# A spectral filter with a mixture of experts on one core: the first forward step in full precision, the bias as matmuls, an earlier first table

## The chip, the core and the metric

One core of a Trainium2 chip runs the whole kernel in one launch. The metric is device microseconds of that core. In the text TensorE is the matmul engine (PE; PEld is its weight load), VectorE is DVE, ScalarE is ACT, GpSimd is POOL and SyncE is SP, which here only issues DMAs.

## What is computed

The input x is (8, 2496, 256) in float32. The first half is a spectral filter along the sequence, the second a mixture of 8 experts in which each token goes to the one expert of the highest score.

```python
X = np.fft.rfft(x, axis=1)
Yr = Xr @ w_r - Xi @ w_i + b_r
Yi = Xr @ w_i + Xi @ w_r + b_i
Y = soft-threshold of Yr and Yi by 0.01
x = irfft(Y).reshape(19968, 256)
expert = argmax(x @ w_gate);  gate = softmax weight of that expert
out = gate * (relu(x @ w1[expert]) @ w2[expert])      # w1: 256 x 1024, w2: 1024 x 256
```

## The kernel before, in words

The transform of length 2496 = 39 x 64 is done as matmuls in two steps. `fwd_a` (line 279) does the 39-point step: per batch eleven pieces of 117 rows (the last of 78) by 512 columns, whose results `ae` go to a DRAM tensor `spec` and come back turned (`turn`, line 300, tile `t1`). `fwd_b` (line 307) does the 64-point step for one of ten slots of a batch, into PSUM tile `pb`. `halves` (line 317) makes from it the operands of the product with the weights: a high and a low part of float32r type (`sh`, `sl`) of real, imaginary and their sum (`re`, `su`). `mix` (line 333) multiplies by three weight matrices: `pk` (the sum by w_r, shared) and `pm` (two more), six products each since every factor is split into high and low. ScalarE copies `pk` to `k`, GpSimd adds the bias to it (`kb`, line 349), VectorE adds `kb` to `pm` (`v`, line 355). `shrink` (line 358) is the threshold: `r` on ScalarE, four operations `y` on VectorE. `inv_b` (line 374, products `pv`, copies `z`) and `inv_a` (line 387, products `pz`, copies `zh` and `zl`, products `py`, copies `yb`) turn it back; `inv_a` also multiplies by the gate matrix.

Splitting a float32 value means: `xh` is its copy in float32r (ScalarE), `xl` the rest (VectorE); a product of two split values is high by high, low by high, high by low. For batch 0, `fwd_a` takes x and its matrix in float32 as they are; for the others `split_x` (line 269) prepares `xh` and `xl` one slot ahead, and three products follow.

The loop of `spectral` (line 454) goes over 80 slots, ten per batch. In it the order of TensorE, SyncE, ScalarE and VectorE is the order of the program; before it, in the prologue, only that of TensorE and SyncE is, and ScalarE's and VectorE's are chosen by the framework. GpSimd's is chosen by the framework throughout. Slot `it` holds: `fwd_b` and `halves` of slot it+1, `shrink` of slot it-1, `mix` of its own, some `fwd_a` of the next batch (lists `first` and, for the split, `second`), loads of x, and the inverse: `inv_b` from the list `back`, and in slots 2 to 5 of a batch ("turning") three `inv_a` each of the batch before. The inner function `inverse` is called three times in a slot.

Routing is drawn in small steps: `route` (line 558) and `table` (line 638) are generators, and `tick(n)` advances the one at the head of the list `jobs` by n steps. Each step ends at a `yield`. A `route` handles half a batch: logits, argmax, softmax weight, a running count by expert (`scan`, `sb`), a product `pr` with a triangular matrix for the count over rows (line 604), then positions `pos`; its rows go out to the DRAM tensor `xs` by indirect DMAs on GpSimd (`scatter`, line 621), a few per slot by `send`, paced by a dependence on `self.paced`. Between `sb` and `pr` stand four empty steps.

`table` makes the list of tiles of 256 rows, each with its expert. Table 0 is for the first five tiles (EARLY) and is drawn in the last batch after the rows of all batches but one have been counted; table 1 has the rest. SyncE reads them as registers (line 734) for the loads of the experts' weights (line 772) and rows. `finish_last` (line 531) does the inverse of the last batch, with the weights of the first tile being split meanwhile, and tiles 0 to 2 with the remaining routing; `experts_rest` does the others.

Of the kernel before, what the change touches and what calls it, by code (L numbers as in the profile page):

```python
# [10 lines left out]
F32 = mybir.dt.float32  # L11
# [87 lines left out]
class Kernel:  # L99
    def __init__(self, tc, nb, x, w_r, w_i, b_r, b_i, w_gate, w1, w2,  # L100
# [6 lines left out]
        done = (nb - 1) * S  # L107
# [72 lines left out]
    def open_forward(self, st):  # L180
# [8 lines left out]
        self.fh = f.tile([117, 120], F32R, name="fh")  # L189
        self.fl = f.tile([117, 120], F32R, name="fl")  # L190
        self.fer = f.tile([78, 120], F32, name="fer")
        self.feh = f.tile([78, 120], F32R, name="feh")
        self.fel = f.tile([78, 120], F32R, name="fel")
# [4 lines left out]
        self.bias = f.tile([128, 2, D], F32, name="bias")  # L198
# [9 lines left out]
        self.raw = raw  # L208
        for h, b in ((0, self.b_r), (1, self.b_i)):
            nc.gpsimd.dma_start(self.bias[:, h, :], b.rearrange("(o n) -> o n", o=1).broadcast_to((128, D)))  # L210
# [25 lines left out]
    def split_constants(self):  # L236
        nc, f, raw = self.nc, self.f, self.raw
        nc.scalar.copy(self.fh, self.far)
        nc.vector.tensor_sub(self.fl, self.far, self.fh)
        nc.scalar.copy(self.feh, self.fer)  # L240
        nc.vector.tensor_sub(self.fel, self.fer, self.feh)
# [4 lines left out]
        raw = {"r": raw["r"], "d": wd, "s": ws}  # L246
        for nm in ("s", "d", "r"):
            self.wh[nm] = f.tile([128, 2, D], F32R, name="wh" + nm)
            self.wl[nm] = f.tile([128, 2, D], F32R, name="wl" + nm)
            nc.scalar.copy(self.wh[nm], raw[nm])  # L250
            nc.vector.tensor_sub(self.wl[nm], raw[nm], self.wh[nm])
# [17 lines left out]
    def split_x(self, b, q, g):  # L269
        nc = self.nc  # L270
        m = 117 if q < 5 else 78
        xt = self.xg[b, q][:m, g:g + 2, :].rearrange("p g d -> p (g d)")
        xh = self.w.tile([117, 512], F32R, tag="xh", name="xh")
        xl = self.w.tile([117, 512], F32R, tag="xl", name="xl")
        nc.scalar.copy(xh[:m, :], xt)  # L275
        nc.vector.tensor_sub(xl[:m, :], xt, xh[:m, :])  # L276
        self.xs2[b, q, g] = xh, xl

    def fwd_a(self, b, q, g):
        nc = self.nc  # L280
        m = 117 if q < 5 else 78
        raw, hi, lo = (self.far, self.fh, self.fl) if q < 5 else (self.fer, self.feh, self.fel)
        p = self.psi.tile([128, 512], F32, tag="u", name="pa", bufs=4)
        if b:
            xh, xl = self.xs2.pop((b, q, g))
            parts = ((hi, xh), (lo, xh), (hi, xl))
        else:
            parts = ((raw, self.xg[b, q][:, g:g + 2, :].rearrange("p g d -> p (g d)")),)
        for i, (a, v) in enumerate(parts):
            nc.tensor.matmul(p[:120, :], a[:m, :], v[:m, :], start=i == 0, stop=i == len(parts) - 1)  # L290
        ae = self.xp.tile([120, 2, D], F32, tag="ae", name="ae", bufs=5)
# [41 lines left out]
    def mix(self, b, s):  # L333
# [3 lines left out]
        def product(nm, slot, to):  # L337
            i = 0
            for c in range(2):
                for a, ww in ((sh, self.wh), (sh, self.wl), (sl, self.wh)):  # L340
                    nc.tensor.matmul(to, a[:, c, slot, :], ww[nm][:, c, :], start=i == 0, stop=i == 5)
# [6 lines left out]
        kb = self.w.tile([128, 2, D], F32, tag="kb", name="kb", bufs=1)  # L348
        self.paced = nc.gpsimd.tensor_tensor(out=kb, in0=self.bias, in1=k.unsqueeze(1).broadcast_to((128, 2, D)), op=ALU.add)  # L349
# [5 lines left out]
        nc.vector.tensor_add(u, p, kb)  # L355
# [55 lines left out]
    def spectral(self, fwd):  # L411
        nb = self.nb
        self.t1s, self.pbs, self.ss, self.us, self.ys, self.hl, self.xs2 = {}, {}, {}, {}, {}, {}, {}
# [23 lines left out]
        first, second, loads, back = ({i: [] for i in range(-1, n)} for _ in range(4))  # L437
        for b in range(1, nb):
            at = 10 * b - 10
            for i, o in enumerate((1, 1, 2, 2, 3, 3, 4, 4, 5, 5, 6) if b == 1 else (-3, -2, -1, 0, 0, 1, 2, 3, 4, 5, 6)):  # L440
                first[at + o].append((b, *pairs[i]))
                second[at + o - 1].append((b, *pairs[i]))
# [11 lines left out]
        for it in range(n):  # L454
            b, s = todo[it]
            late = b == nb - 1
            half, small = iter(()), iter(())
            if it + 1 < n:
# [3 lines left out]
            if it:  # L462
                small = self.shrink(*todo[it - 1])
                next(small)
            next(half, None)
# [503 lines left out]
```

## Time and profile before

| what | value |
|---|---|
| median of 3 runs | 1668.5 us (1666.49 to 1670.34) |
| the profiled execution | 1668.7 us |
| its span, first to last instruction | 1666.9 us |
| mean granted TensorE clock | 0.974 |
| TensorE busy | 1534.7 us (92%) |
| VectorE busy | 1335.3 us (80%) |
| ScalarE busy | 1116.1 us (67%) |
| GpSimd busy | 617.5 us (37%) |

The span is the time from the first to the last instruction of the program; the execution's own time has 1.8 us around it. Busy TensorE time is the union of matmuls that overlap and whose ends are modelled. Times of rows below are microseconds from the start of the span; a row of a timeline has start, duration, engine, line, operation, result and operands, shape, count, and in brackets the idle time of the engine before it and who ended it.

### The profile page before, as it was taken

How to read it: one execution, taken by the hardware profiler on the slowest of the kernel's cores; microseconds unless marked ns; L12 is line 12 of the kernel's file. 1: busy time of each engine (PE TensorE's matmuls, PEld its weight loads, DVE VectorE, ACT ScalarE, POOL GpSimd, SP SyncE). 2: the span in 40 equal slices, each digit the busy share in tenths (PEclk: the TensorE clock that was granted, in tenths of full speed). 3: DMA queues.
4: the chain of work that ended last, by engine and by line, in shares of the span. 5: the costliest groups of instructions: out<-in, count | busy, mean ns of one | idle time of the engine just before them, and what ended most of it. 6: DMA issues, size and time to landing. Idle time of an engine off the chain costs nothing. (4 is left out here: it accounts for less than half of the span.)

```text
span 1666.9 us, 36023 instructions
## 1 busy us (share of the span) xinstructions
PE 1534.7 (92%) x10880; PEld 1422.8 (85%) x10880; DVE 1335.3 (80%) x2755; ACT 1116.1 (67%) x2334; POOL 617.5 (37%) x462
## 2 busy tenths in 40 slices
PE   5889898988988887779999999999999999999997
PEld 2778787878878886778999999999999999999996
DVE  2678878888888888668888888888888888888886
ACT  2677777676767665546677677677677667677675
POOL 2121626362535345351333333333333333333332
PEclk8899999999999998999999999999999999999998
DMA  8753535353535311324322312312312313213210
GB/s 249 200 145 94 171 98 161 108 156 107 164 95 148 102 57 46 114 65 102 97 50 46 99 47 46 100 46 60 85 46 61 83 46 96 49 46 91 52 46 19
DMA packets 182932, 153.81 MB, mean 92 GB/s; under 512 B 120378, under 2 KB 154080, under 8 KB 182477
## 3 DMA queue, kind: packets, MB, share of 16 engines
q1 hardware_dynamic: 162829, 107.17, 25.6%
q0 software_dynamic: 19904, 44.29, 8.1%
q8 instruction: 88, 1.44, 0.4%
q14 instruction: 111, 0.91, 0.2%
HBM read 243.33 MB, written 66.37 MB: 186 GB/s over the span
## 5 line engine op out<-in xcount | busy, mean ns | idle before, releaser
L892 POOL DMA_INDIRECT out<-o,row x154 | 303.7, 1972 | 571.2 <-DVE o L890 546.1
L882 PE MATMUL po<-h,hh 128*128 128x512 f32 x1312 | 463.4, 397 | 2.7 <-ACT hh L849 2.7
L844 PE MATMUL ph<-xh,l 128*128 128x256 f32 x1312 | 372.0, 284 | 4.4 <-DVE l L785 4.4
L844 PE MATMUL ph<-xh,h 128*128 128x256 f32 x1312 | 372.4, 284 | 0.6 <-ACT h L784 0.5
L844 PE MATMUL ph<-xl,h 128*128 128x256 f32 x1312 | 371.8, 283 | 0.2 <-DVE xl L827 0.2
L849 ACT ACTIVATE hh<-ph 128x512 fp32r<-128x512 f32 x328 | 196.0, 598 | 251.9 <-PE ph L844 232.5
L850 DVE SCALAR_TENSOR_TENSOR hl<-ph,hh 128x512 fp32r<-128x512 f32 x328 | 226.7, 691 | 150.6 <-ACT hh L849 136.5
L879 PE MATMUL po<-h,hl 128*128 128x256 f32 x1148 | 322.6, 281 | 0.2 <-DVE hl L850 0.2
L882 PEld LDWEIGHTS po<-h,hh 128*128 128x128 f32 x1312 | 242.2, 189 | 47.4 <-ACT hh L849 3.0
L844 PEld LDWEIGHTS ph<-xh,l 128*128 128x128 f32 x1312 | 251.9, 192 | 8.4 <-DVE l L785 4.9
L844 PEld LDWEIGHTS ph<-xh,h 128*128 128x128 f32 x1312 | 251.4, 192 | 1.4 <-ACT h L784 0.7
L844 PEld LDWEIGHTS ph<-xl,h 128*128 128x128 f32 x1312 | 251.9, 192 | 0.4 <-DVE xl L827 0.4
L349 POOL TENSOR_TENSOR kb<-bias,k 128x512 f32<-128x512 f32 x80 | 106.1, 1326 | 332.8 <-ACT k L347 289.8
L879 PEld LDWEIGHTS po<-h,hl 128*128 128x128 f32 x1148 | 217.9, 190 | 4.5 <-DVE hl L850 0.5
L624 POOL DMA_INDIRECT xs_dram<-yb,pos x176 | 182.8, 1039 | 82.4 <-issue 43.6
L785 DVE TENSOR_TENSOR l<-r,h 128x512 fp32r<-128x512 f32 x332 | 206.8, 682 | 3.1 <-ACT h L784 3.0
L800 DVE TENSOR_TENSOR h<-r,h 128x512 fp32r<-128x512 f32 x332 | 206.9, 684 | 2.8 <-ACT h L799 2.8
L784 ACT CAST h<-r 128x512 fp32r<-128x512 f32 x332 | 180.7, 618 | 1.8 <-DMA r<-moe_w 1.8
L799 ACT CAST h<-r 128x512 fp32r<-128x512 f32 x332 | 180.4, 618 | 0.0
L368 DVE SCALAR_TENSOR_TENSOR y<-v,r 64x256 f32<-64x256 f32 x320 | 159.7, 499 | 6.1 <-issue 0.8
L381 PE MATMUL pv<-bi,y 128*128 128x128 f32 x640 | 95.3, 288 | 22.5 <-DVE y L368 20.9
L276 DVE TENSOR_TENSOR xl<-x,xh 117x512 fp32r<-117x512 f32 (+1 forms) x77 | 70.4, 926 | 56.5 <-ACT xh L275 54.7
(190 smaller groups left out, 2927.9 us busy)
## 6 DMA issues: line engine op xcount, KB each, us to landing
r<-moe_w SPq DMA_DIRECT2D x178, 512.0 KB
r<-moe_w SPq DMA_DIRECT2D x632, 128.0 KB
spec_dram<-ae SPq DMA_DIRECT2D x88, 240.0 KB
t<-spec_dram SPq DMA_DIRECT2D x160, 128.0 KB
xq<-xs_dram SPq DMA_DIRECT2D x312, 64.0 KB
x<-x SPq DMA_DIRECT2D x40, 384.0 KB
x<-x SPq DMA_DIRECT2D x40, 84.0 KB
xs_dram<-yb,pos POOLq DMA_INDIRECT x176
```

What stands on the lines that cost most here:

```text
L368: nc.vector.scalar_tensor_tensor(out=y[q * 64:q * 64 + 64, kp, :], in0=u[h, q, :], scalar=LAM, in1=r[h, q, :], op0=ALU.add, op1=ALU.min)
L624: i = nc.gpsimd.indirect_dma_start(out=self.xs[:, :], out_offset=bass.IndirectOffsetOnAxis(ap=pos[:n, g:g + 1], axis=0), in_=y[:n, g, 0:XW ...
L784: nc.scalar.copy(hi[:, c, s], v)
L785: nc.vector.tensor_sub(lo[:, c, s], v, hi[:, c, s])
L799: nc.scalar.copy(hi[:, s, :], v)
L800: nc.vector.tensor_sub(lo[:, s, :], v, hi[:, s, :])
L844: nc.tensor.matmul(p[:, i, :], a[:, c, f * 128:(f + 1) * 128], v[:, c, :], start=m == 0, stop=m == 5)
L849: nc.scalar.activation(hh[:, s, :], p, AF.Relu)
L850: nc.vector.scalar_tensor_tensor(out=hl[:, s, :], in0=p, scalar=0.0, in1=hh[:, s, :], op0=ALU.max, op1=ALU.subtract)
L879: nc.tensor.matmul(p[:, :D], hl[:, f - 1, hs], w2[:, f - 1, 0, :], start=False, stop=False)
L882: nc.tensor.matmul(p, hh[:, f, hs], w2[:, f].rearrange("p a d -> p (a d)"), start=f == 0, stop=f == 7)
L892: i = nc.gpsimd.indirect_dma_start(out=self.out[:, :], out_offset=bass.IndirectOffsetOnAxis(ap=at[h], axis=0), in_=o[:, h, :], in_offset=N ...
```

## The change

`fwd_a` takes float32 operands for every batch; `split_x`, its list `second` and the split matrices go. The bias is added by TensorE: `self.bias` becomes float32r with the high part in row 0 and the rest in row 32 of 128 rows, all else zero, and in `mix` a product of `self.ones` (128 x 128 of ones) with it opens each of the two groups of `pm`. `k` is added by VectorE as it is; GpSimd copies one element of it as a mark for the pacing. `ae` has eight buffers in place of five. In turning slots the first `inverse()` of the slot is called ahead of `shrink` and of the second half of `halves`. Table 0 is drawn from all batches but two, from slot 1 of the last batch on in place of slot 6. Between `sb` and `pr` stand five empty steps, in the last batch ten; ahead of the last product of table 1 four in place of one.

```diff
@@ -104,7 +104,7 @@
         self.ntok = nb * S
         self.cap = TT + self.ntok
         self.nt = (self.ntok + E * (TT - 1)) // TT
-        done = (nb - 1) * S
+        done = (nb - 2) * S
         self.early = EARLY if done - E * (TT - 1) > (EARLY - 1) * TT else 0
         self.spec = [self.nc.dram_tensor(f"spec{i}_dram", (120, G, D), F32, kind="Internal").ap() for i in range(2)]
         self.xs = self.nc.dram_tensor("xs_dram", (E * self.cap, XW), F32, kind="Internal").ap()
@@ -186,16 +186,13 @@
         self.psf = self.pool(st, "psf", 1, side="right", space=PSUM)
 
         self.far = far = f.tile([117, 120], F32, name="far")
-        self.fh = f.tile([117, 120], F32R, name="fh")
-        self.fl = f.tile([117, 120], F32R, name="fl")
         self.fer = f.tile([78, 120], F32, name="fer")
-        self.feh = f.tile([78, 120], F32R, name="feh")
-        self.fel = f.tile([78, 120], F32R, name="fel")
         nc.sync.dma_start(far, self.c_fa)
         nc.sync.dma_start(self.fer, self.c_fe)
         self.bm = f.tile([128, K1, 128], F32, name="bm")
         self.bi = f.tile([128, K1, 128], F32, name="bi")
-        self.bias = f.tile([128, 2, D], F32, name="bias")
+        self.bias = f.tile([128, 2, D], F32R, name="bias")
+        self.ones = f.tile([128, 128], F32R, name="ones")
         self.xg = {}
         for q in range(6):
             self.load_x(0, q)
@@ -206,8 +203,10 @@
             nc.sync.dma_start(raw[nm], src.rearrange("(c p) n -> p c n", p=128))
         self.wh, self.wl = {}, {}
         self.raw = raw
+        self.braw = self.w.tile([33, 2, D], F32, tag="y", name="braw", bufs=6)
         for h, b in ((0, self.b_r), (1, self.b_i)):
-            nc.gpsimd.dma_start(self.bias[:, h, :], b.rearrange("(o n) -> o n", o=1).broadcast_to((128, D)))
+            for q in (0, 32):
+                nc.gpsimd.dma_start(self.braw[q:q + 1, h, :], b.rearrange("(o n) -> o n", o=1))
         self.nlam = f.tile([128, 1], F32, name="nlam")
         nc.vector.memset(self.nlam, -LAM)
 
@@ -235,15 +234,19 @@
 
     def split_constants(self):
         nc, f, raw = self.nc, self.f, self.raw
-        nc.scalar.copy(self.fh, self.far)
-        nc.vector.tensor_sub(self.fl, self.far, self.fh)
-        nc.scalar.copy(self.feh, self.fer)
-        nc.vector.tensor_sub(self.fel, self.fer, self.feh)
         ws = self.w.tile([128, 2, D], F32, tag="r", name="wsum")
         wd = self.w.tile([128, 2, D], F32, tag="r", name="wdif")
         nc.vector.tensor_sub(wd, raw["i"], raw["r"])
         nc.vector.scalar_tensor_tensor(out=ws, in0=raw["i"], scalar=-1.0, in1=raw["r"], op0=ALU.mult, op1=ALU.subtract)
         raw = {"r": raw["r"], "d": wd, "s": ws}
+        zero = self.w.tile([128, 2, D], F32, tag="y", name="zero", bufs=6)
+        nc.vector.memset(zero, 0.0)
+        nc.vector.tensor_copy(self.bias, zero)
+        nc.vector.tensor_scalar_add(self.ones, zero[:, 0, 0:128], 1.0)
+        bh = self.w.tile([33, 2, D], F32R, tag="y", name="bh", bufs=6)
+        nc.scalar.copy(self.bias[0:1], self.braw[0:1])
+        nc.scalar.copy(bh[32:33], self.braw[32:33])
+        nc.vector.tensor_sub(self.bias[32:33], self.braw[32:33], bh[32:33])
         for nm in ("s", "d", "r"):
             self.wh[nm] = f.tile([128, 2, D], F32R, name="wh" + nm)
             self.wl[nm] = f.tile([128, 2, D], F32R, name="wl" + nm)
@@ -266,29 +269,13 @@
             self.nc.sync.dma_start(t[lo * j:hi * j, :n, :].rearrange("p g d -> p (g d)"), src)
         self.xg[b, q] = t
 
-    def split_x(self, b, q, g):
+    def fwd_a(self, b, q, g):
         nc = self.nc
         m = 117 if q < 5 else 78
-        xt = self.xg[b, q][:m, g:g + 2, :].rearrange("p g d -> p (g d)")
-        xh = self.w.tile([117, 512], F32R, tag="xh", name="xh")
-        xl = self.w.tile([117, 512], F32R, tag="xl", name="xl")
-        nc.scalar.copy(xh[:m, :], xt)
-        nc.vector.tensor_sub(xl[:m, :], xt, xh[:m, :])
-        self.xs2[b, q, g] = xh, xl
-
-    def fwd_a(self, b, q, g):
-        nc = self.nc
-        m = 117 if q < 5 else 78
-        raw, hi, lo = (self.far, self.fh, self.fl) if q < 5 else (self.fer, self.feh, self.fel)
         p = self.psi.tile([128, 512], F32, tag="u", name="pa", bufs=4)
-        if b:
-            xh, xl = self.xs2.pop((b, q, g))
-            parts = ((hi, xh), (lo, xh), (hi, xl))
-        else:
-            parts = ((raw, self.xg[b, q][:, g:g + 2, :].rearrange("p g d -> p (g d)")),)
-        for i, (a, v) in enumerate(parts):
-            nc.tensor.matmul(p[:120, :], a[:m, :], v[:m, :], start=i == 0, stop=i == len(parts) - 1)
-        ae = self.xp.tile([120, 2, D], F32, tag="ae", name="ae", bufs=5)
+        nc.tensor.matmul(p[:120, :], (self.far if q < 5 else self.fer)[:m, :],
+                         self.xg[b, q][:m, g:g + 2, :].rearrange("p g d -> p (g d)"), start=True, stop=True)
+        ae = self.xp.tile([120, 2, D], F32, tag="ae", name="ae", bufs=8)
         to = ae.rearrange("p g d -> p (g d)")
         if b == 0 and g:
             nc.vector.tensor_copy(to, p[:120, :])
@@ -335,24 +322,25 @@
         sh, sl = self.ss.pop((b, s))
 
         def product(nm, slot, to):
-            i = 0
+            i = 0 if nm == "r" else 1
+            if i:
+                nc.tensor.matmul(to, self.ones, self.bias[:, 1 if nm == "d" else 0, :], start=True, stop=False)
             for c in range(2):
                 for a, ww in ((sh, self.wh), (sh, self.wl), (sl, self.wh)):
-                    nc.tensor.matmul(to, a[:, c, slot, :], ww[nm][:, c, :], start=i == 0, stop=i == 5)
+                    nc.tensor.matmul(to, a[:, c, slot, :], ww[nm][:, c, :], start=i == 0, stop=i == (5 if nm == "r" else 6))
                     i += 1
 
         pk = self.psi.tile([128, 512], F32, tag="yo", name="pk")
         product("r", 2, pk[:, :D])
         k = self.w.tile([128, D], F32, tag="k", name="k", bufs=1)
         nc.scalar.copy(k, pk[:, :D])
-        kb = self.w.tile([128, 2, D], F32, tag="kb", name="kb", bufs=1)
-        self.paced = nc.gpsimd.tensor_tensor(out=kb, in0=self.bias, in1=k.unsqueeze(1).broadcast_to((128, 2, D)), op=ALU.add)
+        self.paced = nc.gpsimd.tensor_copy(self.mark, k[0:1, 0:1])
         yield
         p = self.psf.tile([128, 2, D], F32, tag="m", name="pm", bufs=1)
         product("d", 0, p[:, 1, :])
         product("s", 1, p[:, 0, :])
         u = self.w.tile([128, 2, D], F32, tag="v", name="v")
-        nc.vector.tensor_add(u, p, kb)
+        nc.vector.tensor_add(u, p, k.unsqueeze(1).broadcast_to((128, 2, D)))
         self.us[b, s] = u
 
     def shrink(self, b, s):
@@ -410,7 +398,7 @@
 
     def spectral(self, fwd):
         nb = self.nb
-        self.t1s, self.pbs, self.ss, self.us, self.ys, self.hl, self.xs2 = {}, {}, {}, {}, {}, {}, {}
+        self.t1s, self.pbs, self.ss, self.us, self.ys, self.hl = {}, {}, {}, {}, {}, {}
         self.jobs, self.rows = [], []
         pairs = [(q, g) for q in range(6) for g in ((0, 2) if q < 5 else (0,))]
         todo = [(b, s) for b in range(nb) for s in range(10)]
@@ -434,12 +422,11 @@
         for _ in self.halves(*todo[0]):
             pass
 
-        first, second, loads, back = ({i: [] for i in range(-1, n)} for _ in range(4))
+        first, loads, back = ({i: [] for i in range(n)} for _ in range(3))
         for b in range(1, nb):
             at = 10 * b - 10
             for i, o in enumerate((1, 1, 2, 2, 3, 3, 4, 4, 5, 5, 6) if b == 1 else (-3, -2, -1, 0, 0, 1, 2, 3, 4, 5, 6)):
                 first[at + o].append((b, *pairs[i]))
-                second[at + o - 1].append((b, *pairs[i]))
             for q, o in enumerate((None, None, 0, 1, 1, 2) if b == 1 else (-7, -5, -4, -2, 0, 2)):
                 if o is not None:
                     loads[at + o].append((b, q))
@@ -455,15 +442,11 @@
             b, s = todo[it]
             late = b == nb - 1
             half, small = iter(()), iter(())
+            turning = b and 2 <= s < 6
             if it + 1 < n:
                 self.fwd_b(*todo[it + 1])
                 half = self.halves(*todo[it + 1])
                 next(half)
-            if it:
-                small = self.shrink(*todo[it - 1])
-                next(small)
-            next(half, None)
-            turning = b and 2 <= s < 6
             turns = iter(range(3 * s - 6, 3 * s - 3) if turning else ())
 
             def inverse():
@@ -474,8 +457,15 @@
                     break
 
             spare = 1 if late else 0
+            if turning:
+                inverse()
+            if it:
+                small = self.shrink(*todo[it - 1])
+                next(small)
+            next(half, None)
             self.tick(2 + spare)
-            inverse()
+            if not turning:
+                inverse()
             mix = self.mix(b, s)
             if not turning:
                 next(mix)
@@ -484,8 +474,6 @@
             if turning:
                 next(mix)
             next(small, None)
-            for a in second[it]:
-                self.split_x(*a)
             self.tick(2 + spare)
             inverse()
             next(small, None)
@@ -500,7 +488,7 @@
                 self.write_blank()
             if it + 4 < n:
                 self.turn(*todo[it + 4])
-            if late and self.early and s == 6:
+            if late and self.early and s == 1:
                 self.jobs.append(self.table(0))
         for _ in self.shrink(*todo[n - 1]):
             pass
@@ -598,7 +586,7 @@
         pa = pa[:, 8:, :]
         sb = small("sb", (117, E), BF16)
         nc.vector.tensor_copy(sb, pa[:, GH - 1, :])
-        for _ in range(4):
+        for _ in range(10 if b == self.nb - 1 else 5):
             yield
         p = self.psi.tile([128, 512], F32, tag="yo", name="pr")
         nc.tensor.matmul(p[:117, :E], self.ltri, sb, start=True, stop=False)
@@ -709,7 +697,8 @@
         if last:
             lap = rt.tile([128, 128], F32, name="lap")
             nc.vector.tensor_copy(lap, fin[:, 3:4].broadcast_to((128, 128)))
-            yield "pe"
+            for _ in range(4):
+                yield
             p = self.psi.tile([128, 512], F32, tag="yo", name="pl")
             nc.tensor.matmul(p[:, 0:128], lap, self.ident, start=True, stop=True)
             for h in range(2):
```

## Rows read from the trace of the kernel before

**Rows 1.** Busy time by stage, one row for each stretch: the stretch, its length, then busy us (and instructions) of PE, PEld, DVE, ACT, POOL, the granted clock, the DMA engines' busy share and GB/s.

```profile
0.00:100.00 100.00, 73.71 (x395) 54.55 (x396) 49.01 (x106) 47.49 (x101) 22.12 (x36) 0.90 0.73 214
100.00:578.00 478.00, 418.63 (x3174) 394.33 (x3173) 393.89 (x947) 337.79 (x823) 202.50 (x178) 0.97 0.45 128
578.00:672.00 94.00, 76.83 (x566) 71.80 (x565) 74.29 (x203) 51.95 (x125) 49.23 (x46) 0.92 0.18 56
672.00:757.00 85.00, 68.68 (x441) 62.40 (x441) 56.29 (x160) 44.34 (x103) 34.70 (x46) 0.90 0.28 85
757.00:1667.00 910.00, 896.87 (x6312) 839.75 (x6309) 761.87 (x1340) 634.51 (x1185) 308.95 (x159) 1.00 0.27 64
416.00:422.00 6.00, 5.69 (x28) 5.69 (x28) 4.49 (x11) 3.29 (x9) 4.28 (x4) 0.50 0.62 175
```

**Rows 2.** Waits of PE from 100 to 578 us: who waited for whom, us in total, times, the longest.

```profile
PE pr L604 <- DVE sb L600: 23.0, 6, 3.9
PE pk L341 <- ACT yb L407: 10.9, 18, 1.1
PE pv L381 <- DVE y L368: 10.9, 13, 1.6
PE pz L392 <- DVE zl L398: 7.3, 6, 1.2
PE py L406 <- DVE zl L398: 4.4, 6, 0.7
PE py L406 <- ACT yb L407: 1.8, 6, 0.3
```

**Rows 3.** Timeline of PE from 396 to 425 us.

```profile
404.28 0.28 PE L341 MATMUL pk<-wlr,sh 128*128 128x256 f32 x1
404.40 0.28 PE L341 MATMUL pk<-whr,sl 128*128 128x256 f32 x1
...
404.88 0.40 PE L290 MATMUL pa<-xh,fh 117*120 117x512 f32 x1
...
405.58 1.05 PE L381 MATMUL pv<-bi,y 128*128 128x128 f32 x8
...
407.91 1.06 PE L313 MATMUL pb<-bm,t 128*128 128x128 f32 x8
...
416.31 0.17 PE L604 MATMUL pr<-sb,ltri 117*117 117x8 bf16 x1 [3.94 <-DVE sb L600]
...
417.01 0.41 PE L341 MATMUL pm<-whd,sl 128*128 128x256 f32 x1
417.22 0.41 PE L341 MATMUL pm<-whd,sh 128*128 128x256 f32 x1
```

**Rows 4.** Timeline of all engines from 411 to 418 us, the rows of y, v and kb.

```profile
411.76 0.86 DVE L368 SCALAR_TENSOR_TENSOR y<-v,r 64x256 f32<-64x256 f32 x2
...
413.27 0.63 DVE L355 TENSOR_TENSOR v<-pm,kb 128x512 f32<-128x512 f32 x1
...
416.17 1.87 DVE L368 SCALAR_TENSOR_TENSOR y<-v,r 64x256 f32<-64x256 f32 x2
...
416.46 1.29 POOL L349 TENSOR_TENSOR kb<-bias,k 128x512 f32<-128x512 f32 x1 [2.07 <-ACT k L347]
```

**Rows 5.** Groups of instructions from 100 to 578 us, shapes apart: count, busy us, mean ns of one, idle us of the engine before them and what ended it.

```profile
L368 DVE SCALAR_TENSOR_TENSOR y<-v,r 64x256 f32<-64x256 f32 x242 | 119.0, 492 | 3.4
L349 POOL TENSOR_TENSOR kb<-bias,k 128x512 f32<-128x512 f32 x61 | 80.7, 1323 | 232.5 <-ACT k L347 193.4 <-DVE y L368 35.2 <-issue 3.1
...
L384 ACT COPY z<-pv 128x256 f32<-128x256 f32 x118 | 69.0, 704 | 0.0
...
L276 DVE TENSOR_TENSOR xl<-x,xh 117x512 fp32r<-117x512 f32 x58 | 52.6, 915 | 41.7 <-ACT xh L275 39.9 <-ACT ae L297 1.3
```

**Rows 6.** Timeline of all engines from 0 to 62 us, the prologue.

```profile
8.71 1.95 PE L290 MATMUL pa<-x,far 117*120 117x512 f32 x4 [0.93 <-DMA x<-x]
...
25.06 0.62 ACT L250 CAST whr<-wraw 128x512 fp32r<-128x512 f32 x1 [8.52 <-DMA wraw<-w_r]
...
26.92 0.68 DVE L294 COPY ae<-pa 120x512 f32<-120x512 f32 x1
...
27.66 2.06 PE L290 MATMUL pa<-x,far 117*120 117x512 f32 x2 [6.73 <-DVE ae L294]
```

**Rows 7.** Waits of PE from 0 to 100 us.

```profile
PE pv L381 <- DVE y L368: 9.0, 7, 3.5
```

**Rows 8.** Waits of PE from 578 to 757 us.

```profile
PE pr L604 <- DVE sb L600: 6.5, 2, 4.1
PE ph L844 <- DVE l L785: 4.0, 1, 4.0
...
PE pq L706 <- DVE fin L700: 2.9, 1, 2.9
...
PE pl L714 <- DVE lap L711: 2.1, 1, 2.1
```

**Rows 9.** Timelines of DVE, POOL and SP between 660 and 770 us: the second table, the last row sent to `xs`, the first load that needs both.

```profile
728.55 0.67 DVE L708 CAST tab<-pq 1x512 int32<-1x512 f32 x1
...
747.11 0.91 POOL L624 DMA_INDIRECT xs_dram<-yb,pos  x1 [0.18 <-issue]
...
756.81 1.98 SPq L749 DMA_DIRECT2D xq<-xs_dram  x4
```

## The prediction

> **What bounds the kernel now.** I began with busy time by stage [rows 1]. From 757 to 1667 us, the experts, TensorE is busy 897 of 910 us at clock 1.00, and the diff issues nothing there: that stage keeps its length. Everything lies in the 757 us before. From 100 to 578 us (six batches of some 80 us) TensorE is busy 419 of 478 us, VectorE 394, and the granted clock is 0.97, so 14 us are lost to half clock. Busy matmuls overlap and say little of where TensorE stands still; its list of waits does [rows 2]: per batch one wait of up to 3.9 us for the VectorE cast sb (line 600), then smaller ones for y, yb and zl.
>
> The timeline of TensorE [rows 3] shows what the long wait costs. pr starts at 416.31 us after 3.94 us of idling. Behind it the 256-column products of mix follow each other at 0.21 us (417.01 to 417.22) where it was 0.12 us (404.28 to 404.40): from 416 to 422 us the granted clock is 0.50 [rows 1], 1.2 in place of 2.4 GHz, and the engine had stood idle before the fall. Such a stall is paid nearly twice.
>
> Why is sb late? VectorE executes in order, and it is behind: v, the last step of a slot, starts at 413.27 us [rows 4], though TensorE had gone on to the next slot's pb at 407.91 us [rows 3], 5 us before. Two things hold VectorE up. First, the split of x [rows 5]: xl takes 0.915 us (58 times), and VectorE idles 41.7 us in front of it, because xh on ScalarE stands behind k and ae, which wait for TensorE; together 1.6 us per slot. Second, kb on GpSimd: the pair of y at 416.17 us took 1.87 us, the pair at 411.76 us 0.86 us; beside the slow pair kb ran from 416.46 us for 1.29 us [rows 4]. Over the stage y takes 0.492 us in the mean [rows 5] against 0.43 us (0.86 / 2) without kb: 242 x 0.06 = 15 us.
>
> **The change, part by part.** The sum goes against the profiled execution, 1668.7 us around a span of 1666.9 us; it agrees with the median of the three runs, 1668.5 us.
>
> *Full precision in place of three products.* A split product is three matmuls, 404.88 to 405.58 us, 0.70 us [rows 3]. The full-precision one of batch 0 is two instructions of TensorE: four of them take 1.95 us with the tail of the last [rows 6], so some 0.45 us each and 0.91 us a product, an estimate from that row. Added: 0.21 us for 77 products (11 per batch from 1 to 7), 16 us. Removed per product: xh, xl and the idling before it. An x tile is held one slot longer, until fwd_a; loads into its buffer are issued three slots or more after that, so SyncE's queue waits for nothing new.
>
> *Bias by products.* Two 256-column products of 0.12 us (a spacing that holds each one's weight load) in 80 slots: 19 us on TensorE. kb leaves GpSimd (1.32 us per slot [rows 5]) and the path to v. The 1x1 copy that takes its place as pacing has no row in this stage; it costs between nothing and kb's time, on an engine busy 203 of 478 us [rows 1], and holds up scatters alone.
>
> So TensorE gets 35 us more work, for certain: 20 x 0.12 + 11 x 0.21 = 4.7 us before 100 us, 120 x 0.12 + 64 x 0.21 = 27.8 us from 100 to 578, 2.4 us from 578 to 672. Against it stand the stalls.
>
> *Prologue and batch 0 (to 100 us).* TensorE stands 6.7 us, to 27.66 us, for the sixth ae, which VectorE copied only at 26.92 us, after weight work that waited for ScalarE's copy of 25.06 us [rows 6]. These two engines have no order by hand here; with five buffers the sixth ae has to wait for a store, with eight it has not. I take 5 of the 6.7 us; at worst nothing, since the new order isn't visible. The preparation of zero, ones and bias (some six short instructions) lies in VectorE's idle time before the weights; without that cover it costs 2 us. Two more small DMAs on GpSimd stand in front of loads that nothing needs early. The waits of pv for y (9.0 us [rows 7]) shrink when y stands behind xl no longer: 6 us. Net 4.7 - 5 - 6 = -6.3 us (bounds +5 and -11).
>
> *100 to 578 us.* pr waits 23.0 us [rows 2]. Each slot frees VectorE of xl, of its wait and of part of kb, some 2 us, against a lag of 5 us that grew over several slots; and pr is drawn one step later. I take all of it, 11 of the 14 us of half clock and 8 of the 10.9 us for y. The waits in the slots with the inverse step (10.9 + 1.8 for yb, 7.3 + 4.4 for zl, together 24.4 us) hang on a chain of copies that stays. The first inverse piece now stands ahead of r and sh on ScalarE and of sl on VectorE; it has no DMA, and what it passes has the rest of the slot. I take 9 us. Net 27.8 - 23 - 11 - 8 - 9 = -23.2 us (bounds +28 and -46). What is late next: those copies, and z on ScalarE, four of 0.70 us in the slots with two inverse products [rows 5].
>
> *578 to 672 us.* pr 4.1 us, pq 2.9 us [rows 8], half clock 7.5 us (0.08 of 94 [rows 1]). The early table, all VectorE and TensorE work, moves ahead of batch 6's routing into slots 2 and 3, where VectorE has zl to make: I take 4.1 + 1.5 + 5 us and give back 2 for a new wait there (between nothing and pq's 2.9). Net 2.4 - 10.6 + 2 = -6.2 us (bounds +5 and -12).
>
> *672 to 757 us.* Half clock 8.5 us, the second pr 2.4, pl 2.1, ph 4.0 us [rows 8]. Six more empty steps ahead of pr and three ahead of pl take these two waits away, 4.5 us, and some 4 us of half clock. Behind them the last rows and the second table come some 6 us later. Their cover: the table was ready at 729.2 us, the last row went out at 747.11 us, the first load that needs both at 756.81 us [rows 9]. If that doesn't cover it, it costs up to 3 us; I take 1.5. Net -7 us (bounds +3 and -17).
>
> Sum: -6.3 - 23.2 - 6.2 - 7 = -42.7 us, **1626 us**.
>
> **The rivals.** *More comes back (0.15).* If every kb (61 in the stage, 80.7 us) holds VectorE up for its whole length, several times the 15 us that I count is freed, and the rest of the waits of rows 2 goes too: 15.4 + 2.9 + 3 = 21 us, 1605 us. For it speaks the 1.87 us pair; against it the mean of y, and that kb often falls beside other work. The Trainium skill (SBUF — State Buffer, section Who interferes with whom) says that a VectorE operation with two inputs in SBUF and a GpSimd operation that reads SBUF block each other for a whole instruction. The slow pair agrees with that rule; by it alone the sum would be this rival's.
>
> *The inverse slots set the pace (0.18).* If copies to zl and yb hold TensorE whatever VectorE is spared, those 9 us stay, and with them half of the relief in clock and y (10 us); the prologue keeps its order (5 us), and the last two stages give half (7 us): 1657 us.
>
> *Slower (0.12).* sb is late not for the split but for v, r, y and the routing steps ahead of it in VectorE's order; 394 busy of 478 us speak for it, the 5 us lag that starts at xl's waits against. Then pr keeps its wait and its half clock, the 35 us come on top with 2 for the moved table, and only y (14 us) and the end (3 us) give: 1668.7 + 35 + 2 - 17 = 1689 us. It decides if under 35 us of the some 110 us of stalls named above go.
>
> *The early table does nothing:* the first weights' loads may wait for the last inverse product and not for the table. That is in the sum already, at nought, and moves no chance.
>
> **How the numbers follow.** The forecast has 0.51, the rivals 0.15, 0.18 and 0.12; 0.04 is left within 0.2% (3.3 us, about what a measurement of this kernel can tell from no change). Faster: 0.51 + 0.15 + 0.18 = 0.84. The forecast's own bounds are 1607 to 1647 us. Left out are the far end of the first rival, below 1600 us (0.07), and the slower case, above 1668 us (0.12).
>
> **What would show it.** Right: waits of pr under 1 us; clock 0.99 from 100 us to the end of batch 6, and some 76 us a batch; no wait of pa for ae; v within 2 us of the next pb; y at 0.43 us. Wrong: a wait of pr over 2 us, a wait of several us per batch under another name, or an expert stage of another length than 910 us.

## The result and the profile after

The changed kernel takes 1593.4 us (median of 4 runs, 1589.29 to 1596.27) where the kernel before took 1669.4 in the same session: ratio 0.9544, 95% interval 0.9515 to 0.9572. It is faster by 76 us; 43 were predicted, and the time lies below the range. The profiled execution took 1596.3 us around a span of 1594.4.

Busy time by stage of the kernel after, columns as in [rows 1]. The cuts are events of the work: the first pb of batch 1, the first pb of batch 7, the last pb, the first ph of the experts.

```profile
0.00:88.40 88.40, 71.85 (x399) 52.51 (x400) 41.63 (x97) 40.44 (x87) 15.47 (x38) 0.90 0.79 239
88.40:520.70 432.30, 421.91 (x3230) 388.15 (x3229) 319.14 (x880) 306.09 (x756) 134.07 (x175) 0.99 0.48 141
520.70:592.50 71.80, 61.18 (x486) 58.09 (x485) 56.16 (x182) 43.55 (x110) 26.50 (x34) 0.98 0.19 58
592.50:633.90 41.40, 34.77 (x266) 31.47 (x265) 27.71 (x73) 29.04 (x75) 14.81 (x18) 1.00 0.41 124
633.90:1594.40 960.50, 941.34 (x6591) 879.27 (x6589) 800.68 (x1452) 658.61 (x1232) 338.22 (x198) 0.99 0.26 65
```

In the kernel before the same cuts lie at 100.0, 578.0, 650.2 and 701.5 us. So the stretches changed by -11.6, -45.7, -0.4, -9.9 and -4.9 us: three fifths of the gain are in batches 1 to 6. There TensorE is busy 422 of 432 us at clock 0.99 (before: 419 of 478 at 0.97 [rows 1]) and VectorE 319, no longer 394. TensorE's waits in that stretch (who waited for whom, us in total, times, the longest) answer to [rows 2]:

```profile
PE py L394 <- ACT k L336: 4.8, 6, 1.0
PE pz L380 <- DVE zl L386: 3.7, 1, 3.7
PE pm L327 <- DVE v L343: 1.1, 1, 1.1
PE pr L592 <- DVE scan L582: 0.7, 1, 0.7
```

Before, these waits were 59.4 us, 58.3 of them in [rows 2]. There is left 0.7 for pr and nothing for y or yb; a new one is py for ScalarE's copy k, 0.8 us a batch, and the single zl is a disturbance told of at the end. VectorE's lag itself is gone: v started more than 2 us behind the pb that opens the next slot in 29 of the 60 slots of batches 1 to 6 before, now in 5. The groups of that stretch, as in [rows 5]: y takes 418 ns where it took 492, and GpSimd's 1x1 copy 0.30 us where kb took 1.32.

```profile
L356 DVE SCALAR_TENSOR_TENSOR y<-v,r 64x256 f32<-64x256 f32 x239 | 99.8, 418 | 3.3
...
L337 POOL COPY mark<-k 1x1 f32<-1x1 f32 x59 | 17.9, 303 | 248.2 <-ACT k L336 244.6 <-issue 3.6
```

### The profile page after: what moved, and what is told of

Read it like the earlier page. It is cut to its first block, busy times and chain, and to the rows that moved or that the text cites. A ratio compares the mean times of both kernels' runs of the same rounds, so it can differ in the third digit from the quotient of the medians.

```text
span 1594.4 us, 35844 instructions
## 1 busy us (share of the span) xinstructions
PE 1531.1 (96%) x10963; PEld 1409.5 (88%) x10963; DVE 1245.3 (78%) x2680; ACT 1077.7 (68%) x2257; POOL 529.1 (33%) x462
## 4 chain that ended last, share of the span: by engine, by line
issue 41%; PE 32%; POOL 18%; DVE 4%; ACT 2%; DMA 2%; POOLq 0%; SPq 0%; another core or an unknown queue 0%; DVEq 0%; ACTq 0%
POOL out L881 17%; PE pm L330 7%; PE pz L380 5%; PE pb L300 4%; PE pv L369 4%; PE py L394 4%; PE pa L276 4%; PE pk L330 3%; PE pm L327 1%; DMA wraw<-w_r 1%; POOL xs_dram L612 1%; DVE y L356 0%; DMA x<-x 0%; POOLq L881 0%; ACT yb L395 0%
## 5 line engine op out<-in xcount | busy, mean ns | idle before, releaser
L881 POOL DMA_INDIRECT out<-o,row x154 | 299.0, 1942 | 577.3 <-DVE o L879 537.4
L337 POOL COPY mark<-k 1x1 f32<-1x1 f32 x80 | 24.4, 305 | 356.1 <-ACT k L336 352.5
L356 DVE SCALAR_TENSOR_TENSOR y<-v,r 64x256 f32<-64x256 f32 x320 | 133.7, 418 | 6.1 <-ACT r L350 1.6
L313 DVE TENSOR_TENSOR su<-re,pb 128x256 f32<-128x256 f32 x80 | 33.7, 421 | 93.5 <-ACT sh L312 49.4
L380 PE MATMUL pz<-iw,z 128*120 128x136 f32 x704 | 97.1, 281 | 4.5 <-DVE zl L386 3.7
```

What stands on the lines that cost most here:

```text
L380: nc.tensor.matmul(p[:120, c * 136:(c + 1) * 136], self.z[:, c, 3 * g:3 * g + 3, :].rearrange("p j a -> p (j a)"), self.iw[:, c, :], start ...
L881: i = nc.gpsimd.indirect_dma_start(out=self.out[:, :], out_offset=bass.IndirectOffsetOnAxis(ap=at[h], axis=0), in_=o[:, h, :], in_offset=N ...
```

## The experiments

In the table, "batches 1 to 6" is the time from the first pb of batch 1 to that of batch 7 in the profile. A time in the column "before there" holds for the rows down to the next one: these kernels ran on one chip. The last column is the ratio to the kernel before on that chip.

| kernel | median us | before there | batches 1 to 6 | ratio |
|---|---|---|---|---|
| after (the result) | 1593.4 | 1669.4 | 432.3 | 0.9544 |
| e1 fp32 alone | 1615.7 | 1667.8 | 436.5 | 0.9685 |
| e2 bias alone | 1657.3 | | 464.1 | 0.9925 |
| e3 after, kb back | 1605.9 | | 437.5 | 0.9618 |
| e4 after, idle addition | 1613.4 | | 444.1 | 0.9668 |
| e5 after, old order | 1578.5 | 1662.2 | 424.6 | 0.9504 |
| e6 after, pr as before | 1587.7 | | 424.6 | 0.9555 |
| e7 after, late table | 1571.2 | | 423.7 | 0.9459 |
| e8 after, five ae | 1578.3 | | 423.4 | 0.9491 |
| e9 after again | 1595.2 | 1666.9 | 431.1 | 0.9562 |
| e10 both parts alone | 1618.8 | | 432.6 | 0.9724 |
| e11 bias on VectorE | 1599.5 | | 430.0 | 0.9598 |
| e12 after, idle memset | 1595.4 | | 431.3 | 0.9578 |
| e13 after, third time | 1577.4 | 1661.9 | 423.7 | 0.9484 |
| e14 after, late table | 1573.0 | | 423.7 | 0.9462 |
| e15 after, old order | 1576.9 | | 424.6 | 0.9491 |
| e16 both parts alone | 1597.3 | | 429.5 | 0.9601 |

**One part at a time (e1, e2).**

```diff
 # e1: the kernel before, with fwd_a of the kernel after
-            for a in second[it]:
-                self.split_x(*a)
 # e2: the kernel before, with the bias of the kernel after
-        self.paced = nc.gpsimd.tensor_tensor(out=kb, in0=self.bias, in1=k..., op=ALU.add)
+        self.paced = nc.gpsimd.tensor_copy(self.mark, k[0:1, 0:1])
```

> The kernel before with one part of the change alone: the first forward step in full precision, no split of x; kb, the order of the slot, the buffers of ae and the places of the table and of pr stay as before. Theory V (VectorE's lag comes from xl and from its waiting for xh; once that is gone TensorE sets the pace): most of the gain comes with this part, pr waits fall from 23 us to under 5 us in batches 1 to 6, batches of 72 to 74 us, about 1610 us. Theory K (kb on GpSimd holds VectorE up and delays v): the waits stay, 16 us of products are added and some 15 to 30 come back, 1650 to 1670 us. If the new order in the slots with the inverse step is what removed yb's and zl's waits, those waits (24 us) stay here.

> The kernel before with the other part alone: the bias by two products per slot, kb gone, a 1x1 copy as the mark; x is still split. Theory V: TensorE gets 19 us more, y and v come earlier by what kb cost (15 us), the lag behind xl stays: 1655 to 1680 us with waits of pr near 20 us. Theory K: the waits go with kb, y takes 0.42 us, about 1620 us.

e1 gave 52 us, e2 10.6, both near the times of theory V; but pr keeps 12.4 us in e1, where under 5 were expected, and in e2 y falls to 420 ns while 17.3 us of pr's waits stay, so theory K alone fell. TensorE's waits in batches 1 to 6, first e1:

```profile
PE pr L578 <- DVE sb L574: 9.9, 5, 3.4
PE pk L317 <- ACT yb L383: 9.9, 18, 1.6
PE pr L578 <- DVE scan L568: 2.5, 1, 2.5
PE py L382 <- ACT yb L383: 0.6, 1, 0.6
```

and e2:

```profile
PE pr L616 <- DVE sb L612: 15.3, 5, 3.1
PE pk L354 <- ACT yb L419: 9.7, 18, 1.1
PE pv L393 <- DVE y L380: 3.9, 10, 1.1
PE pz L404 <- issue: 3.9, 5, 0.8
PE pr L616 <- issue: 2.0, 1, 2.0
PE pz L404 <- DVE zl L410: 0.8, 1, 0.8
```

Either part takes away the waits for zl (11.7 us [rows 2]; 0.8 left in e2, beside 3.9 us of pz for which the profile shows no cause); those for yb stay near 10 us with either part alone. Against the added work, 64 x 0.16 = 10 us in e1 and 120 x 0.12 = 14 us in e2, the stretch of 478 us lost 41.5 and 13.9 us. So 52 and 28 us of stalls went, together 80. In kernels with both parts and nothing else (e10 and e16, below) 70 and 73 us go, so the two reliefs add up but for a tenth. e2 also shows a price that the prediction missed:

```profile
L287 DVE TENSOR_TENSOR xl<-x,xh 117x512 fp32r<-117x512 f32 x58 | 39.6, 692 | 44.4 <-ACT xh L286 39.7 <-ACT ae L308 4.4
```

Without kb xl takes 692 ns where it took 915 [rows 5].

**What kb did (e3, e4, e12).**

```diff
 # e3: bias and kb as in the kernel before, all else as after
 # e4: the kernel after, plus
+        self.paced = nc.gpsimd.tensor_tensor(out=kb, in0=self.bm[:, 0:4, :]..., in1=k..., op=ALU.add)
-        self.paced = nc.gpsimd.tensor_copy(self.mark, k[0:1, 0:1])
 # e12: the kernel after, plus
+        nc.gpsimd.memset(idle, 0.0)
```

> The kernel after with kb back on GpSimd in place of the two bias products; all else as after. Theory V: VectorE has room now (busy 320 of 433 us in batches 1 to 6), TensorE loses 19 us of products: 1575 to 1590 us, faster than the kernel after. Theory K: y goes back to 0.49 us or more and v comes later; waits of pr or py for VectorE come back, 1615 us or more.

> The kernel after plus one GpSimd addition per slot, as long as kb and with two operands in SBUF, whose result nothing reads (it takes the place of the 1x1 copy and paces the scatters). It shows what GpSimd beside VectorE costs without kb's place on the way to v. Theory K by blocking: VectorE loses up to 80 x 1.3 us, y over 0.49 us, and the time grows by 15 us or more. Theory V, or theory K by the way to v alone: within 5 us of the kernel after, though y may take 0.49 us.

> The kernel after plus one GpSimd memset of 128x512 per slot, right behind the 1x1 copy, into a tile that nothing reads: GpSimd is busy as with the idle addition but reads nothing from SBUF. If GpSimd's reading is what stops VectorE's operations with both inputs in SBUF: y keeps its 0.42 us and the time is that of the kernel after within 3 us. If any work of GpSimd stops them: y near 0.59 us and 15 us or more slower.

e3 lies between its two theories: 1605.9 us, where 1575 to 1590 or 1615 and more were expected. TensorE has 19 us less to do than in the kernel after and still the time is 12.5 us longer; y takes 591 ns and pr waits 11.4 us in batches 1 to 6 again.

Theory K held in its second form: an addition that nobody reads costs 20 us (1613.4 against 1593.4; here chips differ, but their kernels before by 1.6 us only). y in batches 1 to 6 of e4:

```profile
L358 DVE SCALAR_TENSOR_TENSOR y<-v,r 64x256 f32<-64x256 f32 x241 | 139.6, 579 | 3.3
```

The timeline of e4 shows which operations are stopped:

```profile
301.50 1.82 DVE L358 SCALAR_TENSOR_TENSOR y<-v,r 64x256 f32<-64x256 f32 x2
301.77 1.28 POOL L338 TENSOR_TENSOR kb<-bm,k 128x512 f32<-128x512 f32 x1 [1.62 <-ACT k L336]
...
351.29 1.28 POOL L338 TENSOR_TENSOR kb<-bm,k 128x512 f32<-128x512 f32 x1 [7.61 <-ACT k L336]
...
351.30 0.24 DVE L572 TENSOR_REDUCE mx<-lg 117x11 f32<-117x88 f32 x1
...
351.58 1.02 DVE L573 TENSOR_SCALAR mx<-mx 117x11 f32<-117x11 f32 x1
...
352.52 0.77 DVE L388 TENSOR_TENSOR zl<-pz,zh 120x272 fp32r<-120x272 f32 x2
```

The reduction runs beside the addition in its 0.24 us. The next operation, 11 elements wide, ends at 352.60, when the addition does (352.57). Over the run the 209 y that touch no addition take 418 ns, the 111 that do 910 ns with 686 ns of overlap. That mean again mixes two kinds: 54 of the 111 keep 0.42 us, nearly all of them begun before the addition; the other 57 take 1.38 us in the mean and end 0.28 us behind the addition. The pair at 301.50 us has one of each. The 20 zl with an overlap take 432 ns, as the others do: zl reads one operand from PSUM, y both from SBUF. The Trainium skill (SBUF — State Buffer, section Who interferes with whom) has this rule: two SBUF inputs contend with a GpSimd instruction that reads SBUF and block for its whole length; a reduction does not. The trace agrees for y, zl and the reduction, with the limit that a y begun first mostly runs through. The 11-element operation has one SBUF input and is held all the same, which this rule does not cover.

e12 bears on the other half of that rule. The framework moved all 80 memsets into the first 67 us, so it does not show one per slot, and its time (1595.4 beside 1595.2 us in e9) says nothing of the rule; but where they ran beside y, y kept 0.43 us each (1.73 for four):

```profile
48.00 8.69 POOL L339 MEMSET kb<- 128x512 f32 x15
...
52.92 1.73 DVE L358 SCALAR_TENSOR_TENSOR y<-v,r 64x256 f32<-64x256 f32 x4
```

GpSimd that only writes stopped nothing here.

**The small edits, one undone at a time (e5 to e8).**

```diff
 # e5
-            if turning:
-                inverse()
 # e6
+        for _ in range(4):
-        for _ in range(10 if b == self.nb - 1 else 5):
 # e7
-            if late and self.early and s == 1:      # and done = (nb - 2) * S
+            if late and self.early and s == 6:      # and done = (nb - 1) * S
 # e8
-        ae = self.xp.tile([120, 2, D], F32, tag="ae", name="ae", bufs=8)
+        ae = self.xp.tile([120, 2, D], F32, tag="ae", name="ae", bufs=5)
```

> The kernel after with one part undone: in slots 2 to 5 the first inverse piece stands behind r, sh and sl again, as in the kernel before. Theory O (the new order emptied the inverse slots): the waits for yb and zl (24 us before) come back, those four slots take 37 us or more a batch in place of 36.0, 1600 to 1612 us. Theory V (VectorE and ScalarE, freed of the split and of kb, emptied them by themselves): within 4 us of the kernel after, 1590 to 1597 us.

> The kernel after with four empty steps ahead of pr in every batch, as in the kernel before (five, and ten in the last batch, are undone). Theory S (the later draw hides pr): pr waits 1 us or more twice a batch and half clock comes back, 1600 us or more. Theory V (the lag of VectorE is gone, sb is there in time at either place): waits of pr under 0.3 us each, within 4 us of the kernel after; in the last batch the rows go out earlier, which can give the experts up to 3 us.

> The kernel after with the first table again from all batches but one, drawn in slot 6 of the last batch. By the prediction: pq and its neighbours wait 1.5 to 3 us again and 2 us of a wait in slots 2 and 3 go, so 0 to 4 us slower. If the slot of 15 us in the last batch comes from the early table's 40 VectorE steps, it shrinks to some 9 us here and the kernel is 3 to 6 us faster.

> The kernel after with five buffers of ae in place of eight. The prediction gave the buffers 5 us in the prologue: then pa waits for ae again there and the first pb comes 5 us later, 1597 to 1600 us. If the transfer of the first spectra sets the first pb, it comes at 35 us all the same and the time stays within 2 us of the kernel after.

All four came out at or below the kernel after, on a chip where the kernel before was faster as well. So they are read from their profiles, and from e13 to e16. None changes batches 1 to 6 (423.4 to 424.6 us), and in e6 no wait of pr is among TensorE's there: both theory O and, for these batches, theory S fell. e7 has the best ratio of its chip, 0.9459, so the early table seems to cost time where the prediction had it gain; e14 below shows it on one chip. In e8 pa waits 7.1 us for the store of an ae, as it waited 6.7 us for VectorE's copy of an ae in the kernel before, and the first pb comes later; but batch 1 starts 89.4 us after the beginning, 1 us later than in the kernel after: the buffers are worth 1 us. TensorE's waits in the prologue, e8:

```profile
PE pa L276 <- DMA spec_dram<-ae: 7.1, 1, 7.1
PE pb L300 <- DMA t<-spec_dram: 2.6, 1, 2.6
```

In the kernel after the first pb waits 10.9 us for t instead: the time is spent one step later.

**Both parts alone, and the bias on VectorE (e10, e11), beside the kernel after (e9).**

```diff
 # e10: e1 and e2 together, nothing else of the change
 # e11: the kernel after with the late table and
-        nc.scalar.copy(k, pk[:, :D])
+        nc.vector.tensor_add(kb, self.bias, pk[:, :D]...)      # no bias products; v adds kb
```

> The kernel after once more, unchanged, to stand beside the three below. The slot of 15 us in the last batch lies behind the early table's 40 short VectorE steps and must be there again (12 to 15 us); the one in batch 6 has no such steps beside it, and no other kernel so far showed it: gone here, batch 6 takes 70 us.

> The kernel before with two parts of the change and nothing else: the first step in full precision, and the bias by products. The order of the slot, five buffers of ae, four empty steps, the place of the table are as before. Theory V+K (VectorE's two loads, the split and the blocking by kb, are the whole cause; order, buffers and steps do nothing): batches 1 to 6 take 71.3 us each, no wait of pr over 1 us, and with the table late no slot of 15 us: 10 us or more faster than the kernel after, at most 4 us slower than the kernel after with the late table (ratio to before 0.945 to 0.949). Theory O+S (order and steps carry a share): waits of pr and yb of 5 us or more in batches 1 to 6, ratio 0.955 or more.

> The kernel after with the table late, and the bias added by one VectorE operation that reads pk from PSUM (128x512, some 0.69 us a slot) in place of the two products, of ScalarE's copy k and of any GpSimd addition. Theory V+K (TensorE sets the pace, VectorE has 110 of 425 us left, what cost was the place of kb on GpSimd and not the addition): TensorE's 19 us go and nothing comes back, batches of 68.5 us, 12 to 20 us faster than the kernel after with the late table (ratio to before 0.934 to 0.939). Rival (VectorE's order is full again with 55 us more): waits of pr and zl come back, ratio 0.945 or more.

e9's expectation held for the last batch (a slot of 16.5 us) and fell for the others: batch 6 takes 74.8 us again and batch 5 73.6 (see the end). Theory V+K fell in e10 for the whole kernel (ratio 0.9724) and nearly held for batches 1 to 6 (432.6 us beside 431.1; pr waits 4.7 us, yb 4.2): the rest of its time is lost behind them. e11 fell: TensorE is busy 8 us less than in the kernel after (414.31 of 430.0), and the stretch is no shorter (batches 1 to 4, which late starts hardly touch, take 283.0 us beside e9's 282.9). Its waits now are py for yb 2.9, for kb 1.9, pr for VectorE 4.2 us: the rival's sign. With 0.68 us more per slot VectorE is late again, although it has 77 us to spare; that this lag took all of TensorE's saving is argued from these waits.

**On one chip (e13 to e16).** The kernels are those of e9, e7, e5 and e10.

> The kernel after once more, on one chip with the three below. If the late starts in batches 6 and 7 belong to the chip, they are here exactly when they are in the three below too, and the ratio to before lies between 0.948 (none) and 0.956 (with them). If they belong to the code of the kernel after, they are here whatever the others show.

> The kernel after with the late first table again. If the early table's 40 VectorE steps ahead of zl are what makes the slot of 12 to 16 us in the last batch, that slot takes 8 us here and the kernel is 6 to 10 us faster than e13 on this chip. If the chip was the reason, within 3 us of e13.

> The kernel after with the old order in the inverse slots again. Theory V+K: the four inverse slots take 36.3 us a batch in place of 36.0, so 2 to 3 us slower than e13 over seven batches. Theory O: 10 us or more slower than e13, with waits for yb and zl of 10 us or more in batches 1 to 6.

> The kernel before with the two parts alone again. Batches 1 to 6 take within 8 us of those of e13 in sum (425 to 433 us), so the two parts carry that stage alone; the stretch from the last pb to the first ph takes 10 us or more longer than in e13 (51 to 54 against 41 us), because pr and pq wait there and half clock follows: the empty steps are what shortens it. In all 15 to 25 us slower than e13.

The kernel after takes 1577.4 us there, and the ratio is 0.9484 (0.9465 to 0.9502). The late starts told of at the end are in none of the four. e15 is no slower (0.9491): the order is not what emptied the inverse slots. e16 gives 64.6 of the 84.5 us, so the two parts are three quarters of the gain. By stage, e13 (batches 1 to 6, batch 7, to the first ph, the rest):

```profile
88.50:512.20 423.70, 418.24 (x3230) 385.43 (x3229) 319.40 (x880) 307.37 (x756) 134.34 (x175) 1.00 0.50 144
512.20:580.40 68.20, 61.55 (x486) 59.07 (x485) 56.33 (x182) 43.43 (x110) 26.76 (x34) 0.95 0.20 61
580.40:618.10 37.70, 33.69 (x266) 31.27 (x266) 27.97 (x74) 29.48 (x75) 14.73 (x18) 1.00 0.45 136
618.10:1576.70 958.60, 941.08 (x6590) 879.49 (x6589) 800.50 (x1452) 659.02 (x1232) 341.81 (x198) 0.99 0.26 65
```

and e16:

```profile
88.90:518.40 429.50, 422.44 (x3230) 384.03 (x3230) 320.67 (x882) 309.94 (x758) 132.56 (x177) 1.00 0.49 143
518.40:582.10 63.70, 58.23 (x477) 57.06 (x476) 51.23 (x151) 42.19 (x107) 26.67 (x35) 0.97 0.21 63
582.10:628.70 46.60, 38.32 (x274) 34.53 (x274) 32.68 (x106) 29.55 (x73) 16.59 (x21) 0.92 0.37 113
628.70:1597.00 968.30, 947.06 (x6590) 883.14 (x6589) 800.20 (x1447) 659.87 (x1232) 337.22 (x196) 0.99 0.26 64
```

e16's expectation held in batches 1 to 6 (429.5 us) and in all (19.9 us slower); before the first ph it is 8.9 us where 10 or more were expected. The small edits give 5.8 us in batches 1 to 6, 9.7 behind the first ph and 8.9 before it, where e16's pr and pq wait and the clock is 0.92; e6 alone loses 5.7 there (43.4 us), so the ten empty steps carry most of it. They cost 4.5 us in batch 7: that is the early table. The timeline of e13 there:

```profile
532.99 0.29 PE L394 MATMUL py<-zh,gl 120*117 120x272 f32 x1
...
536.43 0.16 DVE L688 TENSOR_REDUCE fin<-st 128x1 f32<-128x8 f32 x1
536.51 0.78 DVE L386 TENSOR_TENSOR zl<-pz,zh 120x272 fp32r<-120x272 f32 x2
...
537.00 0.57 PE L394 MATMUL py<-zl,gh 120*117 120x272 f32 x1 [3.73 <-DVE zl L386]
...
537.37 0.43 PE L394 MATMUL py<-zh,gh 120*117 120x272 f32 x1
...
537.60 0.43 PE L394 MATMUL py<-zh,gl 120*117 120x272 f32 x1
```

The table's short VectorE steps run from 529.59 us to 536.6 and stand ahead of zl. py waits 3.73 us for it, and behind the stall the products follow each other at 0.23 us: half clock (granted 0.50 from 537 to 542 us). In e14 that slot takes 7.63 us in place of 12.46, batch 7 63.3 in place of 68.2. e14 is the fastest kernel here, 1573.0 us, by 4.4 us; 6 to 10 were expected.

## Why the prediction was wrong

Its direction, its cause and nearly all its signs held: pr's waits came from VectorE's lag, 0.7 us of 23 are left, the clock rose to 0.99, y fell to 0.42 us. The size was wrong, and most of that lies in one step, "100 to 578 us": -23.2 predicted, -45.7 measured, -54.3 where nothing disturbs (e13).

- **The waits in the inverse slots** are the term that failed. "The waits in the slots with the inverse step (10.9 + 1.8 for yb, 7.3 + 4.4 for zl, together 24.4 us) hang on a chain of copies that stays", so 9 us were taken. The chain stayed and the waits went, with the old order too: 3.4 us in e15, on yb alone, still 18 waits as before but of 0.2 us each. In the kernel after yb's are gone as well, and py waits 4.8 us for k in their place. For zl, which is VectorE's work, either part is enough (e1, e2); for yb, ScalarE's copy, both are needed (9.9 and 9.7 us with one). That yb's waits too came from VectorE's lag is argued, not shown.
- **kb's price** was read from one row. 15 us for y; xl's 0.915 us held another 58 x 0.22 = 13 us, put down to the split. In TensorE's time e2 gives 28 us. The rule behind the rival "more comes back" holds for y and xl, whose inputs are both in SBUF, but not for every kb and every operation; that rival's 1605 us was the nearest of the four numbers, at a chance of 0.15. Its case against itself, that y's mean is low, mixed 52 y of 912 ns with 268 of 419 (whole run of before).
- **Half clock and y** were discounted (11 of 14, 8 of 10.9). In e13 all of it came: no such stalls, clock 1.00; in the kernel after, the late starts keep some 3 us of half clock.
- **The cost of a stop** had no term. A matmul's record lasts 0.28 us where the next starts 0.12 us later [rows 3], so at a stop the list of waits misses the difference. An estimate from the starts of TensorE's matmuls: at the 56 stops of before in batches 1 to 6, 68 us are lost, where the waits add up to 59.4. So e13 could gain more than the bound of -46, which was made of waits and half clock.
- **The added work** was 24.6 us, not 27.8: a full-precision product takes two spacings of 0.43 us, 0.86 in place of 0.91.
- **Prologue and batch 0**: -11.6 against -6.3, for another reason. ae's buffers gave 1 us, not 5, and the first pb comes 3.5 us earlier in all. Batch 0 itself lost 8.1 us, since its slots no longer split batch 1's x: e1 alone starts batch 1 at 88.6 us.
- **578 to 757 us**: -17.4 against -13.2, by the prediction's own end of it, the first load of xq (682.14 us in the kernel after, 756.81 before). The early table's "new wait" was priced at 2 us with 2.9 as its upper end; it is 4 to 5 us with its half clock. The last steps gave more than thought.
- **The expert stage** was to keep its 910 us and nearly did: from the first load of xq it takes 912.3 us in the kernel after, 909.2 in e14, 915.9 in e16. By the cut at the first ph, with the early steps in it, it moves between 953.5 us (e14) and 968.3 (e16). TensorE's instructions are the same and its busy time is not (937 to 947 us), so this is waiting and half clock in the first steps. What sets it was not followed up.

The stalls of [rows 2] were judged one by one, each by its own releaser. 45.6 of the 58.3 us end at steps of one late engine, VectorE; that engine was made early, and nearly all of them went together.

## What to carry to other kernels

When one engine that works in order is behind, its waits appear under many names; price the relief from the sum of all waits that end at its work, or behind it, and the half clock with them. Compare an operation's mean with its duration when nothing runs beside it: a mean of 0.915 us was 0.69 us and a collision. Room on an engine is no licence to put work there: 0.68 us a slot on VectorE (e11), or seven us of small steps ahead of one urgent one (the early table), gave nothing or cost 4.4 us, whatever the idle share suggests.

## What the runs showed of the hardware

An addition on GpSimd held up VectorE operations that began while it ran until its own end: y and xl, with both inputs in SBUF, and an 11-element operation of 0.17 us with one, which took 1.02 us (e4). Reductions, operations with an input in PSUM and a cast of 8 columns (0.17 us beside the addition in e1) ran through, and so did most y that began before the addition. And in some profiles ScalarE and VectorE started late after matmuls. In the kernel after, batch 6:

```profile
460.95 1.05 PE L300 MATMUL pb<-bm,t 128*128 128x128 f32 x8
...
465.61 0.69 DVE L343 TENSOR_TENSOR v<-pm,k 128x512 f32<-128x512 f32 x1 [4.53 <-PE pz L380]
...
466.36 0.37 ACT L311 COPY re<-pb 128x256 f32<-128x256 f32 x1 [5.67 <-PE pz L380]
```

re reads pb, whose last record ends at 462.00, and starts 4.4 us later; TensorE then waits 3.7 us for zl and falls to half clock (granted 0.50 from 468.6 to 474 us). In 8 profiles (e5 to e8, e13 to e16), on chips where the kernel before takes 1662 us, re never starts more than 1.5 us after both pb's end and ScalarE's own last work; in all others, where it takes 1667 to 1669 us, it does from 1 to 4 times. The kernel after takes 17.7 us of span more with them than without (1594.4 against 1576.7 in e13): 8.6 in batches 1 to 6 and 3.6 in batch 7, where late starts of re lie, and 5.5 elsewhere, which was not traced. This fits its ratio of 0.954 to 0.956 on the one sort of chip and 0.948 on the other. The DMA engines were nearly full in that slot of batch 6 (0.89 to 0.96 from 460 to 466 us), in others they were not; the cause stays open.
